# Gated linear attention and an MLP on one core: q, k and x transposed by DMA from DRAM planes instead of from SBUF

## The chip, the cores and the metric

The kernel runs on one core of a Trainium2 chip. The metric is device time in microseconds (us) from launch to end; below, "span" is the time from the first to the last instruction of the one execution that the profiler recorded. The engines are TensorE (PE for matmuls, PEld for its weight loads), VectorE (DVE), ScalarE (ACT), GpSimd (POOL) and SyncE (SP), whose queue issues nearly all DMAs.

## The reference

Inputs q, k, v and alpha are float32 of shape (batch 4, heads 8, sequence 768, head size 48); alpha lies between 0.8 and 1. `w_ch1` (384 x 1536) and `w_ch2` (1536 x 384) are float64.

```python
for t in range(S):
    state = alpha[:, :, t, :, None] * state + np.einsum('bhd,bhe->bhde', k[:, :, t], v[:, :, t])
    y[:, :, t] = np.einsum('bhd,bhde->bhe', q[:, :, t], state)
x = y.transpose(0, 2, 1, 3).reshape(B, S, H * D)          # (4, 768, 384)
xn = (x - mean) / np.sqrt(var + 1e-06) * g_ln             # over the last axis
out = x + np.maximum(xn @ w_ch1, 0.0) @ w_ch2
```

## The kernel before

The sequence is cut into 6 chunks of 128 steps; with 4 batches this gives 24 attention units, `attention(c, b)`. A unit takes the logarithm of alpha on ScalarE (L259), sums it over the chunk by a matmul with a triangle (L264, or L480 for two batches at once), forms exponentials on ScalarE (L269, L270), and multiplies q and k by them on VectorE (L278). The products then have time on partitions; the score matmuls (L333 in chunk 0, L496 from chunk 1 on, two batches at a time) need the head index on partitions, so q and k are transposed. The scores are masked on VectorE (L347), the state is updated (matmuls L363, sums on VectorE at L376, gates on GpSimd at L378), and the output y comes from matmuls L387 and L403. It is normalised on ScalarE (L415 to L446) and becomes x; x is transposed as well, into the tile `xT`, which the MLP reads.

The transposing has two forms. In chunks 0 and 1 (`c < BY_DMA`) TensorE does it (L294 for q and k, L453 for x). From chunk 2 on the DMA engines do it. Their transpose moves 16-bit elements, so each float32 is split:

- ScalarE copies the low halves of a tile and then its high halves into a tile `planes` (L309, for k and for q; L462 for x, into `parts`).
- SP issues a transposing DMA from SBUF to SBUF (L319, L466). k's result lands in a tile `turned`, q's in the tile that held its natural form; x's lands in its own natural tile `xn`.
- ScalarE joins low and high halves to float32 again (L324, into the memory of `planes`; L469, into `xT`).

`planes`, `turned`, the MLP's sums and its `u` tiles share one ring of 11 buffers with the tag "sum".

The MLP of chunk 0 is plain (L519 first layer, L531 second layer). From chunk 1 on both layers use products of sums: VectorE forms sums of blocks of x (L781) and of the hidden layer (L617), TensorE multiplies them (L807 first layer, L630 second), and VectorE, ScalarE and GpSimd add the results up. The weights are float64: they are loaded in 12 pieces of 768 KB (L179) and rounded to float32 on VectorE and ScalarE (L189 to L199, L195), w1's six pieces first, then w2's. x is kept in DRAM between its making and the last sum (store L429, load L506); results leave at L510.

The order of all work is a string of characters, `ORDER`. Each character names a generator (one per attention unit, per weight piece, for the loads of alpha, k, q and v, for products, sums, ReLUs and outputs), and each occurrence runs that generator up to its next `yield`. Every engine runs its instructions in the order in which they come out. SP's queue too is in order: an issue that waits holds up all that stand behind it.

Of the kernel before, what the change touches and what calls it, by code (L numbers as in the profile page):

```python
# [9 lines left out]
FP32 = mybir.dt.float32  # L10
# [3 lines left out]
UINT16 = mybir.dt.uint16  # L14
# [2 lines left out]

EPS = 1e-6
BY_DMA = 2
STAGED = 3  # L20

ORDER = (
    "000a0a2bcbc1a2d1bda0caabaadbb3abbfbeaaaba2bc1241cdafbebacaccaddcA3bddabcbdccbaaA"
    "bdddb120cedCccf1fcebAc2ddgcAffhcffeee4ebdcgBadC3dchg5dgYYYdhYgChd0g3fghhhfhZZgBe"
    "ZeBAeif15BZBej4jif2eYYZfgCeYDgDj3YhehEfjj0YYYYfiDZZZZZZhijDZEligfYjiEhCGijfjgYYY"
    "ZZZfkGZiYEYghh4FieYGFZjY3GiZFgeHFZl53gSHjgh0gik1ZgZZiHYJhYjgZIhYgZiJ3Y02ISgiSSSj"
    "mPJkSSgSPSSejInhkijSiHlklIjf31Q42SSj1Kjljj3mnPfLK0lQQkSKfSLkeLSfSlilSWeeQlklg2km"
    "mffSkm0QQhhmQW5kkShkmnnhkPnWeemSlhWkknnkmnmSPQkknlOhkWPXXnjlXPlX1XXXXli5pM02jXiS"
    "MMMM2jSSMjXMMMMMWMSMMMMiikMX1oMnr3lMMnMPMMmMMM4oRinMWnMMlj0opppMM0MMkmMMMkWRkMRR"
    "MMMMnRMoMpMMmRlj3MqMMMmmpllo3pOMMMnMpMMRMoMm4RRolpnnonpnmm1MWWoWMoOmM3MnMMR5ooNR"  # L30
    "MNo2MjNokN0OlpMMoMNioMMMMMpoNNMpoRWMplpiiMNNlllokMoppNNNo1ppiMrlMMNWMMMmMMXMXMrr"
    "qMNMMnMMNNOXXXrnXXMmMXrrtmXmrpOmXXnmn32MMMMMMMMMMoMMMMMMMMMMMMMMrOMMqppqrR31MMqM"
    "MMMMMMMMRRMMMMMMMMMMMMR0MMMRMMMMMMOMMMMppRs4pMq1qMMRRtRtMqqMqoMMR5NMrrqrq2vNrNRR"
    "Nqn0Mq3rMrMMsMMNqpMrNNrnMqNqqqooMNMMpMNMMNNNMMMMo2MNMMNrNXMrmXtMMMMXXXXsuMMqqqrr"
    "rsrXXXXMMMXs31MMMMtMMMMMMMrMMMMMMMMMMMq2tRtMMMMMMrqtMMtMRRMMMMMMMMMMM0M3MMMMMOOO"
    "1qtOMMMMMMM04RsuuMMRM3MwsMMMRRRRMsMssM2MMMM5sssxsvst4NttsttMRvtsNqRtssstNssNNNtM"
    "MtRNNNMMMMtMNussutM1MMMMMNvsutstuMNMuMMMttMNvMMNuNMvrvvtMM3MMMMuvNMXXXXvXXXMMXMM"
    "M5vuvvuuMwOMMvXXMMMvM2Mx1MMMMXMMMxx3MMMMMMMMOxRxRx2xMMMMMMMRxwvvvMMMMMMMMvvMMMMM"
    "MwRvvMMMwxwMuuOwRRMMMMMMMMMMwRRMMRuMMMwwM5wwMwwuRxxxuwuMxRMvNuMxNNNwuxNwwwwNOxRx"
    "NxNNNNNwwwxxMMxxvMuMMMMMMMMMMxuvMMMMMMMwNxuXVXXXXXXXXVMMMMVVVVVVVMVVVVXXVVVVVVVV"  # L40
    "VVVVVVVVVVNNVVVVVVVVVVVVVVVVVVVVVNVVVVVVOVOMMMMRRRRRRMVMMMOORRRNNNMMMNMMMRRRNNNM"
    "MMMNNNNNNMMMMMMMMMMMMMMMMMMMMMNNNMMMMMMMMM"
)


# [1 line left out]
def kernel(  # L47
# [13 lines left out]
    nc = tc.nc  # L61

    B, S, H, D = q.shape
    DM = H * D
    DF = w_ch1.shape[1]
    P = 128
    NCB = S // P
    NP = H // 2
    R = 64 + D
    NF = DM // P  # L70
# [5 lines left out]
    raw = ctx.enter_context(tc.tile_pool(name="raw", bufs=B // 2))  # L76
    stage = ctx.enter_context(tc.tile_pool(name="stage", bufs=STAGED))
    work = ctx.enter_context(tc.tile_pool(name="work", bufs=2))
    dram = ctx.enter_context(
        tc.tile_pool(name="dram", bufs=B, space=bass.MemoryType.DRAM))  # L80
# [73 lines left out]
    for h in halves:  # L154
        part = consts[h, 2 * P:]
# [17 lines left out]
    def load_weights(i):  # L173
        if i >= len(pieces):
            return
        dst, src = pieces[i]
        if src.dtype != FP32:
            dst = staged[i] = stage.tile(list(dst.shape), INT64, name="ws", tag="ws")
        nc.sync.dma_start(dst, src)  # L179
# [21 lines left out]
    def take_weights(i):  # L201
        if i < STAGED:
            load_weights(i)
            yield
        if pieces[i][1].dtype != FP32:
            yield from round_weights(i)
        yield
        load_weights(i + STAGED)
        yield
# [26 lines left out]
    def qk_of(c, b):  # L236
        return qks[b if c == 0 else b ^ 1 if c == 1 else (b ^ 1) % 3]
# [3 lines left out]
    for at in ats:  # L241
        nc.gpsimd.memset(at, 0.0)

    def words_of(t):
        return t.rearrange("r w p t -> r (w p t)").rearrange("r (d w) -> r w d", w=2)

    x_of, xT_of, hT_of, las, lps_of, qkT_of, aps_of, ob_of = ({} for _ in range(8))


    def attention(c, b):  # L250
# [26 lines left out]
        for n in (0, 1) if whole else (1, 0):  # L277
            nc.vector.tensor_mul(qk[:, n], raws.pop(("qk"[n], c, b)), (eq, lv)[n])  # L278
            if n == 0:
                row = dram.tile([2, 2 * 64 * NP], FP32, name="row", tag="row")  # L280
# [4 lines left out]
        if not whole:  # L285
            at = at.rearrange("k p i s t -> k (p i s t)")[:, b // 2 * NP * P:][:, :NP * P].rearrange(
                "k (p s t) -> k p s t", s=2, t=HS)
        if c < BY_DMA:
            kT, qT = (work.tile([R, NP, 2, HS], FP32, name=f"{n}T", tag="sum", bufs=11)
                      for n in "kq")  # L290
            for i in range(2):
                tps = ps.tile([R, NP, P], FP32, name="tps", tag="bank", bufs=8)
                for p in range(NP):
                    nc.tensor.transpose(  # L294
                        tps[:, p], qk_of(c, b)[:, i, p].rearrange("p a b -> p (a b)")[:, :R], ident)
                yield
                tv = tps.rearrange("r p (s t) -> r p s t", s=2)
                if i:
                    (nc.vector.tensor_copy if whole else nc.scalar.copy)(out=kT, in_=tv)
                else:  # L300
                    nc.scalar.copy(out=qT, in_=tv)
                    qkT_of[c, b] = kT, qT
                yield
        else:
            planes, turned = [None, None], [None, None]
            for n in (1, 0):
                planes[n] = work.tile([P, 2, NP, P], UINT16, name="planes", tag="sum", bufs=11)
                natural = qk_of(c, b)[:, n].rearrange("t p i c -> t (p i c)").bitcast(UINT16)
                nc.scalar.copy(out=planes[n].rearrange("t w p r -> t w (p r)"),  # L309
                                      in_=natural.rearrange("t (d w) -> t w d", w=2))  # L310
                turned[n] = natural.rearrange("t (w p r) -> t w p r", w=2, p=NP)
                yield
            qT, kT = (t.rearrange("r w p t -> r (w p t)").bitcast(FP32)[:R].rearrange(
                "r (p s t) -> r p s t", p=NP, s=2) for t in planes)
            qkT_of[c, b] = kT, qT
            for n in (1, 0):
                if n:
                    turned[n] = work.tile([P, 2, NP, P], UINT16, name="turned", tag="sum", bufs=11)
                nc.sync.dma_start_transpose(  # L319
                    turned[n].rearrange("r w p t -> r (w p) t"),  # L320
                    planes[n].rearrange("t w p r -> t (w p r)"))
                yield
            for n in (1, 0):
                nc.scalar.copy(out=words_of(planes[n]),  # L324
                               in_=turned[n].rearrange("r w p t -> r w (p t)"))
                yield
        if whole:
            aps = [ps.tile([P, NP, 2, HS], FP32, name=f"aps{i}", tag="bank", bufs=8)
# [17 lines left out]
        else:  # L346
            nc.vector.copy_predicated(  # L347
                out=at.rearrange("k p s t -> k (p s) t"),
# [35 lines left out]
        for p in range(NP):  # L384
# [4 lines left out]
            for n in range(0 if whole else 8):  # L389

                if odd:
                    inner, s, i = n // 4, n // 2 % 2, n % 2
                    r = i
                else:
                    i, s, r = n // 4, n // 2 % 2, n % 2
# [17 lines left out]
        if odd:  # L413
            for r in range(2):
                act(out=x[:, r * DM // 2:][:, :DM // 2], func=AFT.Copy, accum_out=few[:, 4 + r:5 + r],  # L415
                    in_=yps[r][:, r].rearrange("t b d -> t (b d)"))
# [14 lines left out]
        xn = work.tile([P, DM], FP32, name="xn", tag="row", bufs=9)  # L431
# [15 lines left out]
        yield  # L447
        if c not in xT_of:
            xT_of[c] = work.tile([P, NF, B, P], FP32, name="xT", tag="xT")
        if c < BY_DMA:  # L450
            xps = ps.tile([P, NF, P], FP32, name="xps", tag="bank", bufs=8)
            for f in range(NF):
                nc.tensor.transpose(xps[:, f], xn[:, f * P:(f + 1) * P], ident)  # L453
            yield
            if whole:
                nc.vector.tensor_mul(xT_of[c][:, :, b], xps,
                                     g_col.unsqueeze(2).broadcast_to([P, NF, P]))
            else:
                nc.vector.tensor_copy(out=xT_of[c][:, :, b], in_=xps)
        else:  # L460
            parts = work.tile([P, 2, NF, P], UINT16, name="parts", tag="row", bufs=9)
            nc.scalar.copy(out=parts.rearrange("t w f c -> t w (f c)"),  # L462
                                  in_=xn.bitcast(UINT16).rearrange("t (d w) -> t w d", w=2))
            yield
            halves_of_x = xn.bitcast(UINT16).rearrange("r (w f t) -> r w f t", w=2, f=NF)
            nc.sync.dma_start_transpose(halves_of_x.rearrange("r w f t -> r (w f) t"),  # L466
                                        parts.rearrange("t w f c -> t (w f c)"))
            yield
            nc.scalar.copy(out=xT_of[c][:, :, b].bitcast(UINT16).rearrange(  # L469
                "r f (t w) -> r w f t", w=2), in_=halves_of_x)  # L470
        yield


# [449 lines left out]
```

## Time and profile before

| | |
|---|---|
| median of 3 runs | 417.06 us (415.47 to 417.10) |
| the profiled execution | 414.15 us, its span 412.5 us |
| PE busy | 404.9 us (98%) |
| PEld busy | 354.6 us (86%) |
| DVE busy | 325.6 us (79%) |
| ACT busy | 279.2 us (68%) |
| POOL busy | 161.5 us (39%) |
| DMA queue of SP | 54.58 MB, 52.7% of 16 engines' span |

Busy times are sums over one engine, whose instructions mostly run beside those of the others; a row of instructions gives engine, line, output and input tile, shape, count, total busy time, mean duration, and the idle time ahead of it with what ended it. Clock 1.0 was granted throughout.

### The profile page before, as it was taken

What the parts mean: (1) busy time and instruction counts of PE and PEld (TensorE: products, weight loads), DVE (VectorE), ACT (ScalarE), POOL (GpSimd) and SP (SyncE); (2) the same over time, 40 slices, a digit from 0 to 9 for tenths busy, and PEclk for the clock granted to TensorE, in tenths of its full rate; (3) what the DMA queues carried; (4) which work ended last, traced back from release to release, by engine and by line L of the source; (5) the groups of instructions that cost most, each with busy time, mean ns of one, the idle gap of its engine ahead of it and who ended that gap; (6) DMA issues with size and microseconds to landing.
All of it is one profiled execution on the core that took longest, in us unless ns stands there. A gap on an engine that the chain in (4) does not pass through costs nothing.

```text
span 412.5 us, 11425 instructions
## 1 busy us (share of the span) xinstructions
PE 404.9 (98%) x4580; PEld 354.6 (86%) x4580; DVE 325.6 (79%) x626; ACT 279.2 (68%) x572; POOL 161.5 (39%) x180
## 2 busy tenths in 40 slices
PE   8899999999999999999999999999999999999996
PEld 6778888766688889998899988899988899989996
DVE  4499988999999779977688965698876587758673
ACT  6897699999975897596776366859647978123200
POOL 4250200230119551437651356821436801277313
PEclk9999999999999999999999999999999999999999
DMA  6994999694882693366271228817556324100201
GB/s 195 261 343 96 284 251 348 171 291 116 154 232 59 120 210 69 97 146 211 47 123 21 99 95 216 136 42 127 117 132 110 54 79 95 60 0 2 76 21 57
DMA packets 97372, 55.31 MB, mean 134 GB/s; under 512 B 69756, under 2 KB 93436, under 8 KB 97320
## 3 DMA queue, kind: packets, MB, share of 16 engines
q1 hardware_dynamic: 97288, 54.58, 52.7%
q8 instruction: 36, 0.59, 0.6%
q14 instruction: 16, 0.13, 0.1%
q0 software_dynamic: 32, 0.00, 0.0%
HBM read 34.29 MB, written 8.74 MB: 104 GB/s over the span
## 4 chain that ended last, share of the span: by engine, by line
PE 89%; DMA 5%; ACT 3%; issue 1%; DVE 1%; SPq 0%; DVEq 0%; ACTq 0%
PE ops L630 31%; PE hps L807 30%; PE ops L531 8%; PE hps L519 8%; PE yps L403 4%; DMA vn<-in_v_dram 3%; PE aps L496 2%; PE ups L363 2%; DMA qk<-planes 1%; PE lps L480 1%; DMA ra<-in_alpha_dram 1%; ACT ws L195 0%; ACT planes L309 0%; ACT la L259 0%; PE tps L294 0%
## 5 line engine op out<-in xcount | busy, mean ns | idle before, releaser
L646 POOL TENSOR_TENSOR ob<-ob,u 128x192 f32<-128x192 f32 x40 | 25.1, 638 | 69.4 <-DVE ob L643 46.9
L807 PE MATMUL hps<-sum,w 128*128 128x256 f32 x192 | 47.1, 381 | 0.4 <-ACT x L419 0.4
L378 POOL TENSOR_TENSOR mid<-mid,gate 112x192 f32<-112x192 f32 x20 | 12.6, 635 | 83.9 <-DVE mid L376 48.9
L807 PEld LDWEIGHTS hps<-sum,w 128*128 128x128 f32 x192 | 36.3, 190 | 6.2 <-ACT x L419 0.8
L630 PE MATMUL ops<-w,hT 128*128 128x192 f32 x224 | 40.1, 328 | 0.0
L630 PEld LDWEIGHTS ops<-w,hT 128*128 128x128 f32 x224 | 36.9, 190 | 0.3
L309 ACT COPY planes<-qk 128x1024 uint16<-128x1024 uint16 x32 | 32.7, 1036 | 4.1 <-DVE qk L278 2.3
L807 PE MATMUL hps<-xT,w 128*128 128x256 f32 x136 | 34.4, 380 | 0.0
L858 ACT ACTIVATE hT<-hT 128x512 f32<-128x512 f32 x48 | 28.6, 622 | 8.1 <-POOL hT L829 4.9
L519 PE MATMUL hps<-xT,w 128*128 128x256 f32 x144 | 32.9, 384 | 0.2 <-DVE mid L376 0.2
L531 PE MATMUL ops<-w,hT 128*128 128x384 f32 x96 | 32.5, 491 | 0.0
L519 PEld LDWEIGHTS hps<-xT,w 128*128 128x128 f32 x144 | 26.8, 190 | 4.4 <-DVE mid L376 0.8
L807 PEld LDWEIGHTS hps<-xT,w 128*128 128x128 f32 x136 | 25.8, 190 | 3.5
L630 PE MATMUL ops<-ws,sum 128*128 128x192 f32 x160 | 28.4, 326 | 0.0
L531 PEld LDWEIGHTS ops<-w,hT 128*128 128x128 f32 x96 | 17.7, 190 | 11.1
L640 DVE TENSOR_TENSOR ob<-ops,ob 128x192 f32<-128x192 f32 x50 | 17.3, 352 | 12.2 <-POOL ob L646 3.3
L630 PEld LDWEIGHTS ops<-ws,sum 128*128 128x128 f32 x160 | 26.4, 190 | 0.0
L378 POOL TENSOR_TENSOR st<-st,gate 112x192 f32<-112x192 f32 x16 | 14.5, 915 | 28.2 <-DVE st L376 28.2
L630 PE MATMUL ops<-ws,hT 128*128 128x192 f32 x128 | 23.6, 328 | 0.0
L324 ACT COPY planes<-turned 128x1024 uint16<-128x1024 uint16 x16 | 21.6, 1349 | 2.9 <-DMA turned<-planes 2.8
L324 ACT COPY planes<-qk 128x1024 uint16<-128x1024 uint16 x16 | 21.6, 1347 | 1.6 <-DMA qk<-planes 1.6
L826 POOL TENSOR_TENSOR hT<-hT,u 128x512 f32<-128x512 f32 x8 | 11.1, 1388 | 29.2 <-DVE u L825 29.2
(257 smaller groups left out, 1163.8 us busy)
## 6 DMA issues: line engine op xcount, KB each, us to landing
ws<-in_moe_w_ch_dram SPq DMA_DIRECT2D x12, 768.0 KB
vn<-in_v_dram SPq DMA_DIRECT2D x12, 384.0 KB
kept<-x SPq DMA_DIRECT2D x20, 192.0 KB
ob<-kept SPq DMA_DIRECT2D x20, 192.0 KB
out_dram<-ob SPq DMA_DIRECT2D x19, 192.0 KB
rq<-in_q_dram SPq DMA_DIRECT2D x16, 192.0 KB
rk<-in_k_dram SPq DMA_DIRECT2D x16, 192.0 KB
ra<-in_alpha_dram SPq DMA_DIRECT2D x14, 192.0 KB
```

What stands on the lines that cost most here:

```text
L309: nc.scalar.copy(out=planes[n].rearrange("t w p r -> t w (p r)"), in_=natural.rearrange("t (d w) -> t w d", w=2))
L324: nc.scalar.copy(out=words_of(planes[n]), in_=turned[n].rearrange("r w p t -> r w (p t)"))
L378: nc.gpsimd.tensor_mul(new, new, by)
L403: nc.tensor.matmul(yps[r][halves[s], i, p], of, by, start=not (odd and inner), stop=bool(inner or not odd), skip_group_check=bool(odd))
L519: nc.tensor.matmul(hps, w1[:, j // 2, f, j % 2 * P:][:, :P], xT_of[0][:, f, bs], start=(f == 0), stop=(f == NF - 1))
L531: nc.tensor.matmul(ops_of[b], hT_of[c][:, j, b], w2[:, j], start=(j == 0), stop=(j == NJ - 1))
L630: nc.tensor.matmul(acc, lhs[:, j], rhs[:, j], start=(j == 0), stop=(j == NT - 1))
L640: nc.vector.tensor_add(x, acc, x)
L646: getattr(nc.gpsimd, f"tensor_{op}")(x, x, y)
L807: nc.tensor.matmul(acc[:, i], w, b, start=True, stop=True)
L826: add_late(c4, c4, u2)
L858: nc.scalar.activation(out=x, in_=x, func=AFT.Relu)
```

## The change

From chunk 2 on, the split tiles go to DRAM and are transposed on the way back.

- ScalarE's copies into low and high halves stay.
- SP stores the split tile to a DRAM tile `sent` (`sentx` for x), 128 rows of (low half, high half). Read as 256 rows, (time, half), the low and the high row of one time step lie next to each other.
- The transposing DMA reads these 256 rows and writes 256 16-bit columns per block, so that low and high halves lie adjacent and are float32 as they land. For q and k the result lands in two new tiles `turned` of the ring "sum"; for x it lands in `xT`.
- ScalarE's joins (L324, L469) are gone.
- `ORDER` is another string of the same characters' kind, with additional steps for the stores. The strings are left out below.

Lines after the first edit move by 1 to 6: scores from L496 to L490, first products from L807 to L801, second products from L630 to L624, the second layer of chunk 0 from L531 to L525, the first from L519 to L513.

```diff
 BY_DMA = 2
+X_BY_DMA = 2
 STAGED = 3
...
-    def words_of(t):
-        return t.rearrange("r w p t -> r (w p t)").rearrange("r (d w) -> r w d", w=2)
+    def part(c):
+        return nc.scalar.copy
...
-            planes, turned = [None, None], [None, None]
+            turned, sent = [None, None], [None, None]
             for n in (1, 0):
-                planes[n] = work.tile([P, 2, NP, P], UINT16, name="planes", tag="sum", bufs=11)
+                planes = work.tile([P, 2, NP * P], UINT16, name="planes", tag="sum", bufs=11)
                 natural = qk_of(c, b)[:, n].rearrange("t p i c -> t (p i c)").bitcast(UINT16)
-                nc.scalar.copy(out=planes[n].rearrange("t w p r -> t w (p r)"),
-                                      in_=natural.rearrange("t (d w) -> t w d", w=2))
-                turned[n] = natural.rearrange("t (w p r) -> t w p r", w=2, p=NP)
-                yield
-            qT, kT = (t.rearrange("r w p t -> r (w p t)").bitcast(FP32)[:R].rearrange(
-                "r (p s t) -> r p s t", p=NP, s=2) for t in planes)
-            qkT_of[c, b] = kT, qT
+                part(c)(out=planes, in_=natural.rearrange("t (d w) -> t w d", w=2))
+                yield
+                sent[n] = dram.tile([P, 2, NP * P], UINT16, name="sent", tag="sent", bufs=2 * B)
+                nc.sync.dma_start(sent[n], planes)
+                yield
             for n in (1, 0):
-                if n:
-                    turned[n] = work.tile([P, 2, NP, P], UINT16, name="turned", tag="sum", bufs=11)
-                nc.sync.dma_start_transpose(
-                    turned[n].rearrange("r w p t -> r (w p) t"),
-                    planes[n].rearrange("t w p r -> t (w p r)"))
-                yield
-            for n in (1, 0):
-                nc.scalar.copy(out=words_of(planes[n]),
-                               in_=turned[n].rearrange("r w p t -> r w (p t)"))
+                turned[n] = work.tile([P, NP, 2 * P], UINT16, name="turned", tag="sum", bufs=11)
+                nc.sync.dma_start_transpose(turned[n], sent[n].rearrange("t w d -> (t w) d"))
+                if n == 0:
+                    qT, kT = (t.rearrange("r p t -> r (p t)").bitcast(FP32)[:R].rearrange(
+                        "r (p s t) -> r p s t", p=NP, s=2) for t in turned)
+                    qkT_of[c, b] = kT, qT
                 yield
...
-            parts = work.tile([P, 2, NF, P], UINT16, name="parts", tag="row", bufs=9)
-            nc.scalar.copy(out=parts.rearrange("t w f c -> t w (f c)"),
-                                  in_=xn.bitcast(UINT16).rearrange("t (d w) -> t w d", w=2))
-            yield
-            halves_of_x = xn.bitcast(UINT16).rearrange("r (w f t) -> r w f t", w=2, f=NF)
-            nc.sync.dma_start_transpose(halves_of_x.rearrange("r w f t -> r (w f) t"),
-                                        parts.rearrange("t w f c -> t (w f c)"))
-            yield
-            nc.scalar.copy(out=xT_of[c][:, :, b].bitcast(UINT16).rearrange(
-                "r f (t w) -> r w f t", w=2), in_=halves_of_x)
+            parts = work.tile([P, 2, DM], UINT16, name="parts", tag="row", bufs=9)
+            part(c)(out=parts, in_=xn.bitcast(UINT16).rearrange("t (d w) -> t w d", w=2))
+            yield
+            sent = dram.tile([P, 2, DM], UINT16, name="sentx", tag="sentx", bufs=B)
+            nc.sync.dma_start(sent, parts)
+            yield
+            nc.sync.dma_start_transpose(xT_of[c][:, :, b].bitcast(UINT16),
+                                        sent.rearrange("t w d -> (t w) d"))
```

More of the change, by code (lines that the diff above doesn't have):

```diff
@@ L19 @@
 BY_DMA = 2
+X_BY_DMA = 2
 STAGED = 3
 ORDER = (
[L23 to L40, printed above, removed]
@@ L41 @@
-    "VVVVVVVVVVNNVVVVVVVVVVVVVVVVVVVVVNVVVVVVOVOMMMMRRRRRRMVMMMOORRRNNNMMMNMMMRRRNNNM"
-    "MMMNNNNNNMMMMMMMMMMMMMMMMMMMMMNNNMMMMMMMMM"
+    "002a10ab02ba1bcaad3a2a1acadbd0bbbcbaabAaabbe2cfbbcccccAa1adda4aaaef0bbbdAd1hgb2d"
+    "adcdefcd3dB1f4efbffbfcebAeedae2dbc3hBd5ddhdgdcgBcYCgeYhYdgc0fggfchdehBhhfefgcciY"
+    "YYAjCcC54cgeZZZjCCYZeeYZZZBDDYFZhfFZZZZhYDif33Y1EeigjZhZg2fYe0EfhEjDhYjeYgFij3lk"
+    "FgYYYffiiggZEhijG4ghIgYZhihhljjiYGYiZj31kZZIGHZZZY2SYZIHHGHYIhfZffYg5fjifgggjjji"
+    "khkhhik3flSllgSkkgkPhilJ0llk0khlJQlX3ePee11iKJ2SSeQjSLKPLKeLWSSmWeWXXn2PPPiP0jWP"
@@ new lines @@
+    "jjjWSiii5Skk4SSknQnmSmXm0S3mkSmnmnnnllnmXXQloXjmlknQnkXmp4SSlkk1kS3Q0kOSSkll2QoX"
+    "lkSSSS0p5iiWlpMMMMiMXXnSSMM3MMMMpMjMMMMnlMMMmpM1M2Mpjminllomn1MMMiMMp3o1QnmoMpmW"
+    "ooMkMMMMMM32MmMWMnoWmOMoMnMMMmWnMojjlmlRMMMnMMqMMMMjnRlMMMMMMpp5ooolopWRrmlO4npR"
+    "RRMRRRRRppNNMMNNkjpMMMMMMNONM0riqmWMMMkoMNRMppqo2q0NMMMMMMksijrtNoNN041opmMproNM"
+    "NMWMNMMo22OoXnoMv33MNNXXXXXXMMtMMMMmrMnnXMnMMXpqoXtqMprXMqM13otMMMMMMMMMMMMMMMMt"
+    "tmqprrqrsnnR1MMMMMMMMMMMMMMMMMMMMMMMMMMMMMMMMMMMMMMMMMOrRRRR0ORppq5urqqqqRrrrmsr"
@@ new lines @@
+    "MMOqRRr0RMMmMsr4RNoqqNN1rqqrMppoRN2MMMMMuNNMNMMNNrMurN2NMNpMqMMMNMMMMMssMMMrMMMM"
+    "MNXXXNNtXXXXXXxMMMMM3sMttMqOXXMMMMMrrrMMMMMMMMMMsuMM0MMMOMMMRMOrqRMMMtMMvsRRwMMM"
+    "MMMMMMMMMMMMMMMMMMRMMRMsMMMMMM5MssttstttsMrRsRuRRRMMMt4qtvtNsttqsvsNNNx1sMNN2N3M"
+    "O3ssMuMstttsssqMqMMMRMMMMMNttMsNNNNMxtxxvNMtuvxMMMMMMNMMMNNvMMMMMMMXvXXMXvXXMXX3"
+    "uMXMMMMMMMwMMMMXOvMMMMMMMMMMMuXMRRMMM2uMRMMMMM5uxRuv1uuvvwvvwwxwwMMMMMMMMMMMuuvR"
+    "vwRxvMMMxMwMMMMuwuMMMMMuuMuuRMMRu5xvwx3xRwwxvwwMMMMvMxMRNNRMxOvvMwNvxOOwxNvNNNNx"
@@ L43 @@
+    "xuxwwwwwNxxwxMMMMNMMMMMMMMwRNxMMMMMNNMMMMXXXXVMXXVMXMMVOXXOXXVVVVVVVVVVVVVVVVVVV"
+    "VRVVVVRMRVRRVVVVRVNVNNVVVVVVVVVVVVVVVVRRVVVVVVVVRNNNRNVMMMMMMMMRMMOMNNNNNNMOMVRN"
+    "MNMMMMMMMNMMMMMMMMMMMMNMMMMMNNMMMMMMMMMMMM"
 )
@@ L449, in attention @@
             xT_of[c] = work.tile([P, NF, B, P], FP32, name="xT", tag="xT")
-        if c < BY_DMA:
+        if c < X_BY_DMA:
             xps = ps.tile([P, NF, P], FP32, name="xps", tag="bank", bufs=8)
```

## The prediction

> **What bounds the kernel now.** I read the page first, then what the matrix engine waited for, then the chain, then the rows of the tiles that change.
>
> ```profile
> span 412.5 us, 11425 instructions
> PE 404.9 (98%) x4580; PEld 354.6 (86%) x4580; DVE 325.6 (79%) x626; ACT 279.2 (68%) x572; POOL 161.5 (39%) x180
> GB/s 195 261 343 96 284 251 348 171 291 116 154 232 59 120 210 69 97 146 211 47 123 21 99 95 216 136 42 127 117 132 110 54 79 95 60 0 2 76 21 57
> q1 hardware_dynamic: 97288, 54.58, 52.7%
> ```
>
> PE is busy for 98% of the span, ScalarE (ACT) for 68%. Busy PE alone proves little, so I look at what PE waited for, in all:
>
> ```profile
> PE ups L363 <- DMA vn<-in_v_dram: 1.7, 2, 1.1
> PE lps L216 <- DVE more L213: 1.1, 1, 1.1
> PE aps L496 <- ACT planes L324: 0.7, 1, 0.7
> PE hps L807 <- ACT x L419: 0.4, 1, 0.4
> PE hps L519 <- DVE mid L376: 0.2, 1, 0.2
> ```
>
> That is 4.1 us, of which ScalarE ended 1.1 and its joins (L324) 0.7. The chain gives the pace of matmuls when nothing waits; its last column counts records, and an f32 matmul leaves two:
>
> ```profile
> 41.28 10.63 PE hps L519 x48
> 60.58 0.81 PE lps L480 x8
> 66.39 1.09 PE aps L496 x64
> 79.18 0.33 PE xps L453 x3
> 97.24 5.16 PE ops L531 x16
> 146.13 4.84 DMA qk<-planes
> 151.05 1.34 ACT planes L324
> 180.93 24.17 PE hps L807 x112
> 409.28 0.36 DVE ob L640
> ```
>
> 24.17 us for 56 matmuls of L807 is 0.43 us each; 10.63 for 24 of L519 is 0.44; 5.16 for 8 of L531 is 0.65. The matmuls follow each other to 409.2 us, and 3.3 us of sum and store follow. The change takes no matmul away and adds none, so the time moves only by what it does to PE's waits: a gain is bounded by the 4.1 us above. The Trainium skill (Trainium Kernel Development and Optimization, Performance Expectations) calls matmul busy time a bad metric and prefers that of weight loads; by that rule PE, with 86%, has more room than 2%. That is a rival below.
>
> **The joins that go.**
>
> ```profile
> L309 ACT COPY planes<-qk x32: 1028/1037/1052, 47.8 to 321.7; 128x1024 uint16<-128x1024 uint16 x32
> L324 ACT COPY planes<-turned x16: 1332/1350/1370, 56.4 to 326.2; 128x1024 uint16<-128x1024 uint16 x16
> L324 ACT COPY planes<-qk x16: 1331/1348/1369, 63.0 to 327.4; 128x1024 uint16<-128x1024 uint16 x16
> L469 ACT COPY xT<-xn x16: 1042/1058/1067, 153.9 to 348.0; 128x768 uint16<-128x768 uint16 x16
> L429 SPq DMA_DIRECT2D kept<-x x20: 319/388/534, 70.6 to 338.7; - x20
> ```
>
> 32 x 1.35 + 16 x 1.06 = 60 us of ScalarE go, 21% of its busy time. The copies that split into planes (32 x 1.04 us, L309) stay. On PE's path lies only one place: a transpose that took 4.84 us, a join of 1.34, then the scores. I take off the 0.7 us of that wait, and the 0.4 for L419 too, as ScalarE's queue grows shorter: **-1.1 us**; if the copies that stay (L309) made the latter, it is -0.7. What is late next is the transpose's landing.
>
> **The stores that come.** 32 of 256 KB and 16 of 192 KB make 11.5 MB on top of 54.58. At the queue's own pace (52.7% for 54.58 MB) its share grows to 64%. SP issues 48 more, at 0.39 us (L429) 19 us, in a queue where each transpose now also waits until its store has landed; loads of q, k, v and alpha for later blocks and gate rows stand behind it. No row shows a store of 256 KB to its landing. The nearest:
>
> ```profile
> 403.06 6.94 SPq L510 DMA_DIRECT2D out_dram<-ob  x4
> 106.55 1.23 SPq L319 DMA_TRANSPOSE qk<-planes  x1
> 109.78 1.37 ACT L324 COPY planes<-qk 128x1024 uint16<-128x1024 uint16 x1 [0.63 <-DMA qk<-planes]
> ```
>
> The last store of 96 KB is issued by 410.0 and the span ends at 412.5: at most 2.5 us. In the built order of the changed kernel the stores stand 1.2 to 49 us of PE work ahead of their transposes, 20 of the 48 under 4; with 2.5 to land, SP may wait up to 1.3 us here and there, and the loads behind have more lead than that. I take 0 for PE, with 0 to 2 us as bounds.
>
> **The transposes, now from DRAM.** Count and bytes are the same. One from SBUF landed 3.2 us after its issue (106.55 to 109.78); with other traffic, 146.13 to 150.97, 4.84. From DRAM none is shown: as bounds I take 2.4 (3.2 less 0.84, if its issue of 1.23 is as short as a copy's 0.39) and 6.4 (twice 3.2); I expect 3.2 to 4.0, by the undisturbed row, since the scores waited once only, with a join of 1.35 on top. What covers it is the PE work between a pair's last transpose and its scores in the built order, counted in matmuls at the paces above: 17 of L519 make 7.6 us, and 14 of L531 with shorter ones 11.7, for the two pairs of the first block; 4 of L531 with shorter ones 4.4, and 15 of L807 6.6, in the next; 7 and 13 of L807, 3.1 and 5.7, in the third; 10 and 9, 4.4 and 4.0, in the last. The one of 3.1 waits for a matmul six places further back and may be issued there: 5.7. So with up to 4.0 us all are hidden. With 4.84, waits of 0.4, 0.4 and 0.8 show, 1.6 in sum; with 6.4, the sum is 2.0 + 2.0 + 2.4 + 0.7 + 0.7 = 7.8. The four chunks of x have 10.9, 9.3, 9.3 and 4.6 us before the first sum on VectorE reads them. I take **+0.3**. The Trainium skill (DMA: Bandwidth & Descriptors, Why small descriptors are slow (HBM only)) speaks against this change: SBUF to SBUF pays nothing for short packets, while a 256-byte one at HBM loses 27%. By it 3.2 us would become at most 4.1 (an estimate), still hidden but for 0.1; no run here shows it yet.
>
> Each batch also draws four buffers instead of three from the ring "sum" of 11, as q's transpose no longer lands in its own natural tile; that is why late transposes wait for a product or for GpSimd.
>
> **The new order.** It moves all work, and at the start it costs something. First uses of weights:
>
> ```profile
> 38.99 0.96 DVE L197 SCALAR_TENSOR_TENSOR ws<-ws 128x768 int32<-128x768 int32 x1 [0.85 <-ACT ws L195]
> 39.99 0.96 DVE L199 SCALAR_TENSOR_TENSOR w<-w,ws 128x768 f32<-128x768 f32 x1
> 95.14 0.96 DVE L199 SCALAR_TENSOR_TENSOR w<-w,ws 128x768 f32<-128x768 f32 x1
> L191 DVE SCALAR_TENSOR_TENSOR w<-ws,w 128x768 f32<-128x768 uint32 x3 | 3.2, 1061 | 0.1
> L442 DVE TENSOR_SCALAR xn<-ob,few 128x384 f32<-128x384 f32 x4 | 2.3, 574 | 0.0
> L456 DVE TENSOR_TENSOR xT<-xps,small 128x384 f32<-128x384 f32 x4 | 2.1, 552 | 0.0
> L193 DVE TENSOR_SCALAR ws<-ws 128x768 int32<-128x768 int32 x3 | 2.0, 668 | 0.1
> L189 DVE TENSOR_SCALAR w<-ws 128x768 int32<-128x768 int32 x3 | 1.7, 555 | 0.9 <-DMA ws<-in_moe_w_ch_dram 0.9
> 40.00:70.00 30.00, 29.84 (x469) 25.13 (x461) 27.49 (x44) 22.92 (x44) 4.41 (x8) 1.00 0.99 284
> 70.00:100.00 30.00, 30.00 (x291) 19.49 (x290) 29.48 (x50) 28.41 (x61) 5.36 (x4) 1.00 0.83 223
> ```
>
> The second piece of w1 was rounded at 40.95 us (39.99 + 0.96) and read at 41.28, after PE's wait of 0.2: no slack. In the new order 6 matmuls of L519, 32 of L496, 4 of L480 and 3 of L453 fewer precede that read: 2.7 + 1.1 + 0.8 + 0.3 = 4.9 us earlier. VectorE has one each of L189, L191, L193, L442 and L456 less to do before it (0.56 + 1.06 + 0.67 + 0.57 + 0.55 = 3.4, some 3.0 as they overlap at their ends), and its wait of 0.85 for L195 need not come back: 3.9. The rest, 1.0, is a wait of PE; bounds 0 and 1.9 with that 0.85. I take **+1.2** with the 0.2 that was there already counted off and 0.4 for VectorE starting the first piece earlier than its load may land.
>
> The last piece of w2 was ready at 96.10 and read at 98.5 (97.24 + 2 x 0.65), 2.4 us of slack. The new order reads it 3.5 us of matmuls sooner and gives VectorE 4.0 us less before it: slack 2.9. But in 40 to 70 us the DMA engines are busy 99%, and in 70 to 100 VectorE 29.48 of 30: a load late by 3 us shows. I take 0, bounds 0 and 4.
>
> The second load of v has 3 x 384 KB more ahead of it, at the 343 GB/s of the third slice 3.4 us, and is read 3.3 us later: its wait grows by 0.1. With what other small reshuffles bring, **+0.4**.
>
> **The sum.** -1.1 + 0.3 + 1.2 + 0.4 = +0.8 us. The profiled execution took 414.15 us, 1.65 around its span; with +0.8 it is 415.0. The median of the three runs shown is 417.06, 2.9 above the profiled one, so I carry the difference over to it: **417.9 us**.
>
> **The rivals.** *The round trip is late* (slower). One mechanism: store, landing and transposing load follow each other, and SP stands in line for each. It decides once issue to landing exceeds 4.0 us; at 6.4 the sum is 7.8 us and the time about 425.6. For it: the 4.84 under traffic, and 11.5 MB more traffic; against it: no join behind, and most leads above 5. Chance 0.18.
>
> *Weights and loads are late in the first 100 us* (slower). The stage above, with DMA at 99% and VectorE at 98%, slips by the upper bounds 1.9 and 4 less what overlaps: +4, 421. Chance 0.17.
>
> *The holes are filled* (faster). The new order brings none of the waits back and takes v's 1.7 and the 0.2 off too: 4.1 less the 1.1 of the start, -3.0, 414.1. For it: ScalarE has 60 us to spare; against it: the starts of both orders are alike. Chance 0.14.
>
> *PE is not the bound* (faster). PE runs below its own speed because operands come late, and a freer ScalarE hands them over earlier. Then all 4.1 us of waits go, and the 72 matmuls of L519 run at L807's pace, 72 x 0.011 = 0.8: -4.9, 412.2. The paces speak against it: they hardly differ between a stage with waits and one without. It is what the Trainium skill's rule on weight loads, named above, would allow. Chance 0.03.
>
> *The change does what it says but is hidden altogether*, 0 +/- 1: this lies within my forecast, which has 0.48 in all, from -1 to +3.
>
> **How the numbers follow.** About 0.5% (2.1 us) is what a measurement of this kernel can tell from no change; the limits are 415.0 and 419.1. Faster: 0.14 + 0.03 = 0.17. Slower: 0.18 + 0.17 of the two slow rivals, and 0.05 of the forecast's upper end: 0.40. Same: the other 0.43 of the forecast. The range leaves out the freer PE, half of the filled holes and half of the late round trip (0.03 + 0.07 + 0.09): 414.0 to 424.0.
>
> **What would show it.** Right: PE's waits stay under 6 us in sum, the first at the second piece of w1; scores wait for no transpose by more than 1 us; ACT's busy time falls to about 220 us; DMA grows to about 64%. Wrong: PE rows that wait at L490 (the scores' new line) for a transpose, or at the second layer of the first block for w2; transposes whose issue to landing is over 4 us; or a PE pace of L807 below 0.43 us. If the scores wait at each of the eight pairs, the round trip is the cause; if the loss lies before 100 us, the order is.

## The result and the profile after

The changed kernel takes 418.36 us (median of 20 runs, 416.19 to 421.10), the kernel before 416.44 (20 runs, 414.42 to 418.07). The ratio is 1.0048, 95% interval 1.0029 to 1.0067: 2.0 us slower, 1.2 to 2.8. (A ratio leaves out the few executions that ran slower as a whole, so it can differ a little from the quotient of two medians.) The forecast was 417.9 out of a sum of +0.8. The profiled execution took 418.96 us. That of the kernel before, with 414.15, was quicker than all of its 20 runs, so the two profiles lie 4.8 us apart where the medians lie 1.9 apart. From the page after:

```profile
span 417.3 us, 11438 instructions
...
PE 405.6 (97%) x4580; PEld 356.6 (85%) x4580; DVE 328.7 (79%) x626; ACT 228.0 (55%) x524; POOL 166.6 (40%) x180
...
q1 hardware_dynamic: 104200, 66.12, 61.1%
```

ScalarE's busy time fell by 51 us (279.2 to 228.0) and the span still grew by 4.8. What PE waited for, after (us in total, times, the longest):

```profile
PE aps L490 <- DMA turned<-sent: 2.0, 1, 2.0
PE xps L449 <- ACT xn L442: 1.6, 2, 0.9
PE xps L449 <- DVE xn L438: 1.4, 1, 1.4
PE lps L217 <- DVE small L218: 1.1, 1, 1.1
PE tps L295 <- DVE more L279: 0.7, 1, 0.7
PE hps L513 <- ACT kT L300: 0.7, 1, 0.7
```

With three more of 0.2 to 0.3 the sum is 8.2 us where it was 4.1. The waits for v, for the planes' join and for L419 are gone; in their place stand one wait for a transpose from DRAM and several for rows and small tiles of the first two blocks, which no step of the forecast named. By stage, the table of windows, after and then before. After the window and its length each row gives the busy time of PE, PEld, DVE, ACT and POOL, then PE's granted clock, the DMA share and GB/s:

```profile
0.00:100.00 100.00, 94.15 (x1240) 73.71 (x1241) 81.62 (x139) 77.30 (x179) 20.95 (x34) 1.00 0.88 244
100.00:140.00 40.00, 37.79 (x627) 28.46 (x626) 35.85 (x71) 21.98 (x53) 14.99 (x12) 0.96 0.86 219
140.00:350.00 210.00, 209.73 (x2363) 193.91 (x2362) 164.32 (x328) 117.27 (x270) 99.61 (x101) 1.00 0.61 149
```

```profile
0.00:100.00 100.00, 96.87 (x1312) 74.98 (x1313) 85.19 (x150) 84.37 (x185) 22.01 (x36) 1.00 0.85 242
100.00:140.00 40.00, 40.00 (x589) 31.41 (x588) 36.90 (x66) 31.80 (x69) 14.90 (x14) 1.00 0.53 128
140.00:350.00 210.00, 208.87 (x2358) 192.35 (x2357) 161.40 (x328) 151.35 (x296) 96.75 (x100) 1.00 0.51 113
```

PE is busy 2.7 us less by 100 us and 2.2 less from 100 to 140, and in that stage its mean clock is 0.96; from 140 to 350 it wins 0.9 back. The chain of the second stage, after:

```profile
116.61 1.30 SPq L317
...
118.00 4.53 DMA turned<-sent
...
122.66 1.72 PE aps L490 x64
```

The chain runs through SP. Its timeline (start, duration) has the four transposes of this stage in one stretch:

```profile
113.87 6.32 SPq L317 DMA_TRANSPOSE turned<-sent  x4
```

The last of them is issued at 118.0 and lands 4.5 us later, and the scores follow. They take 1.72 us for 64 records; in the chain before the change 64 took 1.09. Narrow windows of the same trace show why:

```profile
120.00:123.00 3.00, 1.02 (x63) 0.93 (x59) 2.93 (x5) 1.92 (x7) 1.13 (x1) 1.00 0.92 216
123.00:126.40 3.40, 3.40 (x67) 2.92 (x59) 3.33 (x7) 0.00 (x0) 0.00 (x0) 0.54 1.00 349
```

Behind PE's wait of 2.0 us the clock is granted at half for 3.4 us, which costs some 1.7 us more (3.4 x 0.5). So this one wait costs 3.7 us of the profiled execution. The halved clock is not in every run: 9 of the 20 had a mean clock of 0.999 or more and a median of 416.89 us, the other 11 (0.992 to 0.996) one of 419.14.

### The profile page after: what moved, and what is told of

Its sections match the earlier page's. It is cut to its first block, busy times and chain, and to the rows that moved or that the text cites. A ratio compares the mean times of both kernels' runs of the same rounds, so it can differ in the third digit from the quotient of the medians.

```text
span 417.3 us, 11438 instructions
## 1 busy us (share of the span) xinstructions
PE 405.6 (97%) x4580; PEld 356.6 (85%) x4580; DVE 328.7 (79%) x626; ACT 228.0 (55%) x524; POOL 166.6 (40%) x180
## 3 DMA queue, kind: packets, MB, share of 16 engines
q1 hardware_dynamic: 104200, 66.12, 61.1%
## 4 chain that ended last, share of the span: by engine, by line
PE 85%; DVE 6%; ACT 5%; DMA 2%; issue 1%; SPq 1%; DVEq 0%; ACTq 0%
PE hps L801 32%; PE ops L624 30%; PE hps L513 7%; PE yps L399 4%; PE ups L359 2%; PE aps L490 2%; PE ops L525 2%; PE lps L474 1%; DVE sum L775 1%; DMA rq<-in_q_dram 1%; DMA turned<-sent 1%; PE lps L265 1%; DVE ws L584 1%; ACT planes L310 1%; PE aps L329 1%
## 5 line engine op out<-in xcount | busy, mean ns | idle before, releaser
L640 POOL TENSOR_TENSOR ob<-ob,u 128x192 f32<-128x192 f32 x40 | 27.8, 704 | 82.3 <-DVE ob L637 62.0
L801 PE MATMUL hps<-sum,w 128*128 128x256 f32 x192 | 46.9, 380 | 0.0
L801 PEld LDWEIGHTS hps<-sum,w 128*128 128x128 f32 x192 | 36.4, 190 | 5.0
L624 PE MATMUL ops<-w,hT 128*128 128x192 f32 x224 | 39.8, 326 | 0.0
L310 ACT COPY planes<-qk 128x1024 uint16<-128x1024 uint16 x32 | 32.3, 1041 | 10.8 <-DVE qk L279 7.4
L624 PEld LDWEIGHTS ops<-w,hT 128*128 128x128 f32 x224 | 37.0, 190 | 0.3
L374 POOL TENSOR_TENSOR mid<-mid,gate 112x192 f32<-112x192 f32 x20 | 15.2, 774 | 52.0 <-DMA gate<-row 30.2
L801 PE MATMUL hps<-xT,w 128*128 128x256 f32 x136 | 34.6, 381 | 0.0
L513 PE MATMUL hps<-xT,w 128*128 128x256 f32 x144 | 32.4, 382 | 0.7 <-ACT kT L300 0.7
L525 PE MATMUL ops<-w,hT 128*128 128x384 f32 x96 | 32.3, 489 | 0.0
L513 PEld LDWEIGHTS hps<-xT,w 128*128 128x128 f32 x144 | 26.9, 190 | 5.0 <-ACT kT L300 0.8
L374 POOL TENSOR_TENSOR st<-st,gate 112x192 f32<-112x192 f32 x16 | 16.2, 1015 | 33.6 <-DVE st L372 33.6
L801 PEld LDWEIGHTS hps<-xT,w 128*128 128x128 f32 x136 | 25.6, 190 | 3.5
L624 PE MATMUL ops<-ws,sum 128*128 128x192 f32 x160 | 28.6, 327 | 0.0
L525 PEld LDWEIGHTS ops<-w,hT 128*128 128x128 f32 x96 | 17.8, 190 | 11.3
L624 PEld LDWEIGHTS ops<-ws,sum 128*128 128x128 f32 x160 | 26.4, 190 | 0.1
L624 PE MATMUL ops<-ws,hT 128*128 128x192 f32 x128 | 23.5, 327 | 0.0
L624 PE MATMUL ops<-more,sum 128*128 128x192 f32 x120 | 22.0, 326 | 0.0
L624 PEld LDWEIGHTS ops<-ws,hT 128*128 128x128 f32 x128 | 21.2, 190 | 0.1
```

Of the source, the lines that this page charges most:

```text
L310: part(c)(out=planes, in_=natural.rearrange("t (d w) -> t w d", w=2))
L374: nc.gpsimd.tensor_mul(new, new, by)
L513: nc.tensor.matmul(hps, w1[:, j // 2, f, j % 2 * P:][:, :P], xT_of[0][:, f, bs], start=(f == 0), stop=(f == NF - 1))
L525: nc.tensor.matmul(ops_of[b], hT_of[c][:, j, b], w2[:, j], start=(j == 0), stop=(j == NJ - 1))
L624: nc.tensor.matmul(acc, lhs[:, j], rhs[:, j], start=(j == 0), stop=(j == NT - 1))
L640: getattr(nc.gpsimd, f"tensor_{op}")(x, x, y)
```

## The experiments

Theory A at the start: the way through DRAM costs only where no PE work covers it, and the new order is what covers it. Rival B: the way is covered in any order, and the loss is the new order's own, in the first 100 us. The converse, the old transposes in the new order, was not run, so the new order has no test of its own.

**The path in the old order.** The changed code with the old string of turns:

```
 ORDER = ( "002a10ab...  ->  "000a0a2b...  (the string of the kernel before)
```

> The changed kernel's way through DRAM for q, k and x, in the order of the kernel before: each store takes the step of a transpose, each transpose the step of a join. So the transposes come later against their scores than in the changed order: by the matmuls between the last transpose and the first score the eight pairs have 0.9, 1.3, 1.1, 3.9, 4.6, 1.7, 2.4 and 5.0 us. Theory A (the path costs only where it is not covered, and the new order is what covers it): at 3.4 us from issue to landing, waits of 2.5, 2.1, 2.3, 1.7 and 1.0 show at the scores, 9.6 us, and some more if PE comes back at a lower clock after each: 426 us or more, against 416.4 before. Theory B (the path is covered anyway, and the loss of the change is the new order's own in the first 100 us): 416.4 to 417.0, under the 418.4 of the changed kernel.

Measured: 463.67 us, ratio 1.1115 (1.1084 to 1.1146). PE's waits, and SP's for ScalarE's splits, in this run and then in the kernel before:

```profile
PE aps L490 <- DMA turned<-sent: 22.7, 7, 6.7
PE hps L801 <- DMA xT<-sentx: 4.5, 1, 4.5
SPq L313 <- ACT planes L310: 34.3, 14, 7.4
```

```profile
SPq L319 <- ACT planes L309: 12.3, 8, 4.0
```

B falls: the way is not covered in every order. A has the place right, seven waits at the scores, but not the size: 22.7 us instead of 9.6, and x waits too. The landing is mostly not what A had wrong. From the start of the issue to the last update of its semaphore a transpose of q or k took 3.5 us here (median of 32, worked out from the trace); only at the first pair did the last one take 5.5. They were issued late. At the fourth pair, whose lead A had counted as 3.9 us, PE was free at 171.3 us and the last transpose was issued at 171.5. SP's queue had been held up: by stores that wait for a split (34.3 us in all, and 12.3 for transposes that wait for one in the kernel before), and at the first pair by transposes that wait 4.6 us for matmuls of L513. The mean clock of this trace, 0.963 over 458.0 us, adds to the loss.

**Only q and k, and only x, in the old order.** The blocks of the changed `attention` for q and k, or for x alone, put into the kernel before:

```
 q, k:  sent[n] <- planes;  turned[n] <- transpose(sent[n])      | x as before
 x:     sent <- parts;      xT_of[c][:, :, b] <- transpose(sent) | q, k as before
```

> Order of the kernel before; only q and k go through DRAM (32 stores of 256 KB), x is turned from SBUF and joined on ScalarE as before. Theory A: the scores wait as with all three, since they alone are short of cover: within 1 us of that run, some 426 us. Theory B: 416.4 to 417.0. Were the traffic and SP's queue the price instead, two thirds of the loss of the run with q, k and x would show here and a third with x alone.

> Order of the kernel before; only x goes through DRAM (16 stores of 192 KB), q and k as before. Nothing waits for x sooner than 4.6 us after its transpose. Theory A and theory B: 416.4 within 0.5 us. If traffic and SP's queue are the price: a third of the loss of the run with all three, so 3 us if that is 426.

Measured: 449.46 us, 1.0769 (1.0723 to 1.0816), and 430.03 us, 1.0312 (1.0275 to 1.0348). Of the 46 us of both, q and k make 32 and x 13: 69% and 28%, nearly two thirds and one third by the number of transfers. That is the pattern which the expectation named for traffic and SP's queue as the price. A's 0 for x is wrong; PE's waits with x alone:

```profile
PE hps L809 <- DMA xT<-sentx: 4.5, 1, 4.5
PE hps L809 <- DVE sum L783: 2.9, 1, 2.9
```

**ScalarE's work put back.** In the changed kernel, behind each split:

```
+    again = natural.rearrange("t (d w) -> t w d", w=2)   # for x: xn.bitcast(UINT16)
+    nc.scalar.copy(out=again, in_=again)
```

> The changed kernel, and ScalarE does 48 copies more of the size of the joins that went: after each split into planes it copies the natural tile onto itself, in the joins' strided form (32 of 128x1024 and 16 of 128x768 halves, some 60 us of ScalarE in all, at 1.35 and 1.06 each). They stand where the planes are made, not where the joins stood. Theory A (ScalarE's work was off PE's path, so its relief brought at most the 1.1 us of the forecast): 418.4 to 419.9 us. Rival (the relief is worth several us, which the rest of the change eats up): 421 or more.

Measured: 449.58 us, 1.0776 (1.0736 to 1.0816), where the changed kernel has 1.0048: 30 to 31 us for 57 us of copies (ACT 228.0 to 284.9). Theory A missed by all of that. PE's waits are now spread over many partners:

```profile
PE hps L805 <- ACT hT L835: 4.1, 2, 3.5
...
PE lps L478 <- ACT la L260: 3.0, 1, 3.0
...
PE aps L494 <- DMA turned<-sent: 2.9, 3, 2.0
```

The new order needs the time that the joins left free. This does not say that the joins were worth 31 us: the copies stand in an order that was made without them. Theory C, that ScalarE's time is worth half a us for each us, was tested next, in the old order.

**The joins cut short, in the kernel before.**

```
-    nc.scalar.copy(out=words_of(planes[n]), in_=turned[n]...)
+    nc.scalar.copy(out=words_of(planes[n])[:, :, :32], in_=turned[n]...[:, :, :32])
-    in_=natural.rearrange("t (d w) -> t w d", w=2)
+    in_=natural.rearrange("t (d w) -> t w d", w=2)[:, 1:].broadcast_to([P, 2, NP * P])
```

> The kernel before, in its own order, with the 32 joins of q and k cut to a sixteenth of their columns (every wait stays, some 35 to 40 us of ScalarE go), and both planes filled with the high halves, at the same number of elements, so that every word stays finite; the rest of the join and the low halves are left out. It measures the term 'the joins go' by itself. Theory A (ScalarE is off PE's path in the kernel before; PE waits 4.1 us in all): -0.7 to -1.5, some 415.5 to 416.5 us beside 417. Theory C (the run with 60 us of ScalarE put back lost 31 us, so ScalarE's time is worth about half a us each): 400 us or less; a gain of more than 4.1 us would speak for it.

Measured: 415.17 us, 0.9937 (0.9915 to 0.9958): 2.6 us less (1.7 to 3.5), for 32 us of ScalarE (ACT 279.2 to 247.1). C falls, and a little more is gained than A expected. The waits for the join are gone; what is left is late for other reasons:

```profile
PE ups L363 <- DMA vn<-in_v_dram: 1.1, 1, 1.1
PE yps L403 <- DMA vx<-in_v_dram: 1.0, 1, 1.0
```

This is the fastest kernel measured here, but it leaves the joins out and is no candidate.

**Idle stores in the kernel before,** issued by SP and then by ScalarE:

```
+    sent = dram.tile([P, 2, NP * P], UINT16, name="sent", tag="sent", bufs=2 * B)
+    nc.sync.dma_start(sent, planes[n]...)       # second run: nc.scalar.dma_start
```

> The kernel before, in its own order, with the 48 stores to DRAM added at the places of the splits, and nobody waiting for them: SP's queue, DMA traffic and the longer life of the split tiles, without the round trip. The forecast's term for the stores: 0, bounds 0 to 2 us. Theory A (only the round trip costs): 417 to 418. Theory B' (traffic and SP's queue cost by themselves, which the old order was not made for): 420 or more, and then a good part of the 46 us that the path lost in the old order is theirs.

Measured: 436.52 us, 1.0448 (1.0408 to 1.0488): +18.7 us for stores on which nobody waits for their data. B' holds against A. One thing is mixed in: the old join writes into the split tile, so it has to wait for the store that reads it. What ScalarE waited for ahead of the joins (us, times):

```profile
  DMA turned<-planes: 17.7, 11
  DMA qk<-planes: 2.1, 2
```

It is the transposes, and no store stands among them. At every join where the trace shows the landing of both, the store had landed first. So the longer hold on the split tile is not what delayed the joins.

> The kernel before with the 48 idle stores in its own order, which took 436.5 us with the stores in SP's queue; now they are issued from ScalarE's. Theory D: most of the 18.7 us go, 417 to 422 us. Theory E: they stay, 433 or more.

Measured: 434.87 us, 1.0390 (1.0347 to 1.0434). Only 2.4 of the 18.7 us go, and E holds. That does not clear SP's queue, since the two traces show different losses of nearly the same size. With the stores in SP's queue the transposes of q and k land as before: medians of 3.4 and 3.5 us from issue to landing, 3.3 and 3.4 in the kernel before. But they are issued 2.8 us later (median of 32, by the matmuls that PE has begun until then). With the stores in ScalarE's queue they are issued 1.0 us later and land after 4.6 to 4.9 us. So by these traces SP's queue is the price in the first run, and mainly the longer landing in the second. The second trace is of the slowest of its six executions, 438.23 us, and why the transposes land later there stays open.

**The stores in the changed order.** Three kernels in which the later blocks' transposes read an old copy, so that none waits for its store: with full stores, with none, and, the last run of all, with thin ones.

```
-    nc.sync.dma_start_transpose(turned[n], sent[n]...)
+    nc.sync.dma_start_transpose(turned[n], firsts[n, b]...)   # c == 2's copy
 no stores:    if c == 2: nc.sync.dma_start(sent[n], planes)
 thin stores:  nc.sync.dma_start(sent[n][:, :, :32], planes[:, :, :32]) where c > 2
```

> The changed kernel in its own order; from the second block by DMA on, the transposes read the DRAM copy that the first such block left, so that no transpose waits for its store (the later blocks' own q, k and x are left out of the products; all stores are made). Theory A (the round trip is what is late in the changed order: one wait of 2.0 us at the scores and the halved clock behind it, some 1.7): 414.5 to 416.5 us beside 418.4. Theory B (the round trip is covered in the changed order; its loss lies at the start and in the waits for x's rows at 77 to 80 us): 418.4 within 0.7.

> As the run with the old copy, and without the 36 stores of the later blocks (their q, k and x left out of the products likewise): what is left is a transpose from DRAM with no store at all. If traffic and SP's queue cost nothing in the changed order: as the old copy within 0.7 us. If they cost: 1 to 3 us less than it.

> As the run with the old copy (no transpose waits for its own store; the later blocks' q, k and x left out of the products), with the 36 later stores cut to 32 of their 512 or 384 columns: every issue on SP and every wait for the split stays, a fifteenth of the bytes goes to DRAM. The run with the old copy and full stores took 1.0056 of before, the one with no stores 0.9987. Theory E (the bytes on the DMA engines are the price): near the latter, 416.5 to 417.7 us where before takes 417.4. Theory F (SP's issues and the longer hold on the split tiles are the price): near the former, 419.0 to 420.3. By the run with the stores in ScalarE's queue, which gained nothing, I expect the first.

Measured: old copy 420.10 us, 1.0056 (1.0033 to 1.0079); no stores 417.29, 0.9987 (0.9967 to 1.0008); thin stores 420.19, 1.0063 (1.0034 to 1.0093). Taking away the wait of a transpose for its own store gains nothing: the round trip is not what is late, A falls here. Taking 36 stores away gains 2.8 us (420.10 to 417.29). Taking most of their bytes away and leaving the issues gains nothing, against what I expected (E); F holds. The time on the DMA engines did fall with the bytes: 59.8% of 419.0 us with full stores, 55.7% of 418.6 with thin ones, 54.6% of 414.9 with none. SP's timeline shows what the stores change, with none and then with thin ones (start, duration):

```profile
109.08 1.96 SPq L140 DMA_DIRECT2D vx<-in_v_dram  x2
111.08 0.52 SPq L284 DMA_DIRECT2D row<-eq  x1
111.70 0.34 SPq L353 DMA_DIRECT2D gate<-row  x1
112.14 5.32 SPq L321 DMA_TRANSPOSE turned<-sent  x4
```

```profile
108.97 2.27 SPq L140 DMA_DIRECT2D vx<-in_v_dram  x2
111.34 0.57 SPq L317 DMA_DIRECT2D sent<-planes  x1
111.96 0.53 SPq L284 DMA_DIRECT2D row<-eq  x1
112.58 0.55 SPq L317 DMA_DIRECT2D sent<-planes  x1
113.23 0.55 SPq L353 DMA_DIRECT2D gate<-row  x1
113.87 1.20 SPq L317 DMA_DIRECT2D sent<-planes  x2
115.16 5.84 SPq L321 DMA_TRANSPOSE turned<-sent  x4
```

SP issues one after another here without a pause. Four stores take 2.3 us of its time (0.57 + 0.55 + 1.20), the other issues slow a little, and the four transposes start 3.0 us later. PE's longest wait for a transpose, without stores and with thin ones:

```profile
PE aps L497 <- DMA turned<-sent: 0.9, 2, 0.7
```

```profile
PE aps L497 <- DMA turned<-sent: 2.9, 1, 2.9
```

The wait of 0.7 us stands at the first pair of batches, at 75.8 us; at the place of the 2.9 only 0.2 is left. Without stores the clock stays full in that trace; behind the 2.9 it is halved for 3.4 us, as in the changed kernel. Over the runs this is no clean cut: a mean clock of 0.996 or less stands in 5 of 12 runs without stores, in 8 of 12 with thin ones and in 10 of 12 with full ones. What the trace cannot part is SP's slots from the stores' wait for ScalarE's splits in the same queue and from the hold on the split tiles, which thin stores keep as well. That SP has no pause here speaks for the slots.

**The stores from ScalarE's queue, in the changed order.**

```
-    nc.sync.dma_start(sent[n], planes)      (and sent, parts)
+    nc.scalar.dma_start(sent[n], planes)
```

> The changed kernel; the 48 stores are issued from ScalarE's own queue, right behind the copy that makes them, not from SP's. Traffic and round trip stay. In the changed kernel SP issues without a gap from 107.9 us, four stores among it, and the four transposes follow at 113.9; PE waits 2.0 us for them. Theory D (SP's queue is the price of the stores: the 2.9 us that leaving them out brought): the transposes come 2 us earlier, the wait at the scores goes, 415 to 416.5 us beside 418.4; ScalarE pays its issues, 48 of some 0.05 to 0.4 us. Theory E (the traffic on the DMA engines, 0.86 to 1.03 busy from 70 to 140 us, is the price): 418.4 within 0.7.

Measured: 421.94 us, 1.0101 (1.0071 to 1.0131), slower than either theory. The four transposes of that stage come later, not earlier. SP's row for them, and PE's wait at the scores behind them:

```profile
114.81 7.22 SPq L317 DMA_TRANSPOSE turned<-sent  x4
```

```profile
PE aps L490 <- ACT x L415: 1.5, 1, 1.5
```

SP waited four times for a store to land there, 2.6 us in all, because ScalarE issues each store in its own turn. The profile puts PE's wait down to ScalarE, which was done at 125.0 us. But the last transpose landed at 125.1, and the scores began at 125.2, so PE would have waited for it as well. The round trip, which the run with the old copy showed to be covered, is late here.

ScalarE's queue is no free place for the stores: each takes 0.34 to 0.41 us of it there. The experiment is no clean test of D, since it moves the cost to an engine for which both PE and the transposes wait.

**One load later.** The third block's second alpha and its logarithm moved behind the four transposes:

```
- ...mXm0S3mkSmnmnnnllnmXXQloXjmlknQnkXmp4...
+ ...mXmS3mkSmnmnnnllnmXXQlXjmlknQnkXm0op4...   (one 0 and one o moved)
```

> The changed kernel with one move in its order: the load of the third block's second alpha (two issues on SP, some 0.6 us, and 192 KB) and its logarithm go behind the four transposes at 113.9 us. Theory D: the transposes come 0.6 us earlier; the wait of 2.0 us falls to some 1.4, and if the clock is then not halved behind it, another 1.7 go: 416 to 418.0. Theory E: the same size from the traffic. Neither: 418.4 within 0.5.

Measured: 426.64 us, 1.0223 (1.0187 to 1.0260). SP's row for the four transposes, and PE's waits:

```profile
113.95 5.38 SPq L317 DMA_TRANSPOSE turned<-sent  x4
```

```profile
PE lps L474 <- ACT la L260: 8.5, 1, 8.5
...
PE aps L490 <- DMA turned<-sent: 0.8, 1, 0.8
```

The transposes start no earlier than in the changed kernel (113.95 us, there 113.87), so D fails at its first step: with the load out of the way, SP waits 1.4 us for a split ahead of one store. At this place SP's slots and the splits bind nearly alike. The logarithm that was moved is needed 8.5 us before it comes; PE reaches the scores so late that it waits for no transpose there. The wait of 0.8 us is another one, at the first pair, at 75.5 us. I had not followed the load to the matmul that uses it. No kernel with the whole computation beat the kernel before.

## Why the prediction was right, and where its steps were not

The time came out within half a us, but in part by luck. The sum of +0.8 lies below the measured 1.2 to 2.8. It was carried over to a median of three runs, 417.06, that 20 runs put 0.6 lower. And the terms cancel. The joins bring -2.6 where the forecast had -1.1, the stores cost +2.8 where it had 0, and the run without stores, at 0.9987 of before, leaves some +2.1 for the transposes and the order, where it had +1.9. (The last is an estimate: -0.5 us and the 2.6 of the joins, which were measured in the other order.)

*PE bounds the kernel, and the time moves only by its waits.* Right. In the two profiles the waits grew from 4.1 to 8.2 us; with 1.7 for the halved clock that makes +5.8 against +4.8 in the span. That a wait costs more than its length was not in the sum.

*The joins go, -1.1.* Too small: cut short in the old order, those of q and k alone bring 2.6 us (1.7 to 3.5), still inside the 4.1 that bounded any gain. That ScalarE is off the path is true of work taken away in the old order, not of work added to the new one.

*The stores, 0 with bounds 0 to 2.* This is the step that failed most. Leaving 36 of 48 out gains 2.8 us, above the upper bound, and it is not the landing for which I bounded it. The stores delay the start of the transposes behind them in SP's queue, by 3.0 us at the place that counts. How much of this is their slots, how much the splits that they wait for, and how much the hold on the split tiles stays open. I had counted 0.39 us for each issue, 19 us in all, and then costed them at nothing because the loads behind have lead. The transposes behind have less.

*The transposes, +0.3.* One pair of eight waits, 2.0 us, as the last of its four lands 4.5 us after its issue and the four are issued over 6.3 us. My leads counted matmuls from the place in the order to the scores, and a landing after that, as if SP issued at that place. This pair's lead, put at 4.4 us, was 2.7: its last transpose was issued at 118.0, and PE was free at 120.7. The landings were longer than forecast too: 4.2 us in the median, and 18 of the 32 passed the 4.0 at which I let the rival decide. Seven pairs stay hidden all the same, so the rival came true at one place of eight. Its price of about 425.6 us was a small slip: with 7.8 in place of 0.3 the sum gives 425.4.

*The second piece of w1, +1.2; w2, 0; v and reshuffles, +0.4.* PE waits nowhere for w1, so this term is wrong as such; w2 is right at 0; the waits for v are gone. What came instead are the waits for xn (3.0), more (0.7) and kT (0.7) in the first 100 us. Without the 1.1 us that the forecast put down to the joins, and without the 2.0 for the transpose, PE's waits went from 3.0 to 6.2 us between the two profiles: +3.2 where I had +1.6 for the order.

*The signs.* PE's waits stayed not under 6 us, and the first was not at w1. ACT came to 228.0 instead of 220, because neighbouring instructions overlap in the record: the sum of their durations did fall by 60 us. DMA came to 61.1% instead of 64%. Landings over 4 us, a sign of being wrong, did occur. "If the loss lies before 100 us, the order is": 2.7 us of PE's busy time lie there, 2.2 behind it, so both causes share it.

*What the skill said against the change.* The rule cited in the prediction (the Trainium skill, DMA: Bandwidth & Descriptors, Why small descriptors are slow (HBM only)) would make transposes from DRAM dearer than from SBUF. Here the time on the DMA engines does not show it. The kernel before with idle stores moves the same bytes with its transposes from SBUF:

```profile
span 435.1 us, 11520 instructions
...
q1 hardware_dynamic: 104200, 66.12, 58.5%
```

58.5% of 435.1 is 254.5 us; 61.1% of 417.3, with the transposes from DRAM, is 255.0. The landing in the old order hardly shows it either: 3.5 us from DRAM, 3.3 to 3.4 from SBUF. The 4.2 of the changed kernel comes with another order.

## What to carry to other kernels

In a kernel whose order is written out, a part has no price apart from the order: the same way through DRAM costs 46 us in the old order and 2 in its own, and 32 us of copies taken from ScalarE bring 2.6 us in the one, while 57 us put back cost 30 in the other. Cost a new DMA by its slot in the queue that issues it and by what it waits for there, and ask which later issue in that queue has the shortest lead. Ahead of moving an issue, follow its data to the matmul that uses it.

## What the runs showed of the hardware

A short idle time of PE can be followed by a halved clock for 3.4 us. It came behind 2.0 us of waiting in the changed kernel, and behind 1.5 us in the run with the stores in ScalarE's queue. In the trace with x alone through DRAM, PE was busy for 3.1 of 6 us, with one wait of 2.9 us, and kept its clock, and lost it at a later place:

```profile
240.00:243.00 3.00, 1.84 (x9) 1.12 (x7) 2.93 (x7) 0.00 (x0) 1.32 (x2) 1.00 0.02 7
243.00:246.00 3.00, 1.28 (x6) 1.15 (x7) 2.97 (x10) 2.37 (x3) 0.00 (x0) 1.00 0.65 222
...
359.50:366.00 6.50, 4.74 (x14) 4.41 (x15) 3.70 (x10) 0.59 (x1) 0.00 (x0) 0.51 0.24 49
```

So the length of the wait alone does not decide. The Trainium skill (TensorE: Matmul & The Clock Gate, What's actually happening) puts the fall of the clock after an idle window of some 3.4 us, in windows that run freely. The length of the halved stretch agrees with that window; an idle time of 2.0 us, well short of it, was enough here.

The issue of one transpose takes SP 1.23 to 2.3 us, in the median some three times as long as that of a store; the minimum, median and maximum of each in the changed kernel:

```profile
L313 SPq DMA_DIRECT2D sent<-planes x32: 332/410/1493, 57.5 to 319.6; - x32
L317 SPq DMA_TRANSPOSE turned<-sent x32: 1226/1300/2315, 65.3 to 325.4; - x32
```
